# Loading and casting the feed-forward weights first, and new due times in the planner of a fused attention and feed-forward kernel

## The chip, the cores and the metric

The kernel runs on one core of one Trainium2 chip. The metric is the device time of one execution in microseconds (us); the time before is the median of three runs. One profiled execution gives the page and the trace, whose span (883.6 us) goes from the first to the last instruction and is some 2 to 3 us shorter than the time.

The engines are named as the profile names them: PE (TensorE, matrix products; PEld its weight loads), DVE (VectorE), ACT (ScalarE), POOL (GpSimd) and SP (SyncE, which here only issues transfers). Each engine runs its own queue in order and waits for the others by semaphores.

## The reference

Eight batches of eight heads, 576 positions, head size 64. For each row of scores only the 32 largest are kept, the softmax is taken over these, and the result, 4608 tokens of 512, goes through a feed-forward layer with a squared ReLU:

```python
scores = scale * np.matmul(q, k.transpose(0, 1, 3, 2))
kth = np.partition(scores, -32, axis=-1)[..., -32:-31]
scores = np.where(scores >= kth, scores, -1e9)
attn = softmax(scores)
x = (attn @ v).transpose(0, 2, 1, 3).reshape(4608, 512)
h = x @ w_in                 # w_in 512 x 2048
out = np.maximum(h, 0) ** 2 @ w_out   # w_out 2048 x 512
```

## The kernel before

**Groups.** A step of attention is a group: 128 query rows of the two heads of a head pair (or, for the last 64 rows of each head, of four heads). There are 144 groups, 18 for each batch. For a group `top_k` and `attend` do the following.

- PE computes scores of two heads against all keys (the helper at line 424, f32) into a PSUM tile of three banks, of which there is one. ACT copies them to an `s` tile (line 533; six buffers).
- DVE finds the 32nd largest score of each row: pairwise maxima (line 589, with an ACT copy of `m` at line 597, and line 599), then rounds of MAX8 and MATCH_REPLACE8 (lines 616 and 620) and a last MAX8 which gives the threshold `kth` (line 623). POOL does integer additions and subtractions for it (line 584).
- ACT computes a penalty `w` (line 631, twice for a group; four buffers). PE transposes the scores and adds the penalty to them in PSUM, in three pieces called flips (`flip`; lines 427 and 424), again in a tile of three banks of which there is one. ACT takes the exponential into `p` (line 665; four buffers).

`collect` multiplies `p` by v (PE), copies (ACT, line 692), takes reciprocals (DVE, line 694), scales (POOL, line 696), transposes (PE) and copies the result into `xt` (ACT, line 720). When four head pairs of 256 rows are there, they form a chunk, which `feed` takes through the feed-forward layer: eight blocks of products with `win` (`fh`), ReLU on ACT (line 746), squares on POOL or ACT (lines 757 and 760), then products with `wo` in four parts for each 128 rows (`fo`), a copy and a store. There are 19 chunks; the last two have 128 rows. In the last chunk DVE squares (line 754).

**Weights.** `win` and `wo` stay in SBUF as bf16. They come as 16 pieces of 512 KB in f32: eight of w_in, then eight of w_out. Each is loaded into one of two `ws` buffers, which lie in the memory of the last eight of the 17 `g` tiles, and then cast by POOL (line 868). Every `fh` and `fo` lists all 16 casts as its dependences (`after=weights`), so that no `g` tile is written before the `ws` buffers are done with.

**The planner.** Nothing of the order is written by hand. Each operation is put into a plan (`pl.op`) with its engine, an estimated duration, a due time (`prio`: the smaller, the earlier it is taken of all that are ready) and what it depends on. `schedule` plays the program with these estimates and fixes the order on each engine, and the buffer of each tile. The due times are built from a nominal time of the group, `tg = T0 + PER*n`, and constants: `LEAD` (how far ahead scores are due), `ME`, `MQ`, `MP`, `MA` (steps of the top-k), `LAG`, `LAGL` and `STEP` (the feed-forward blocks), `LATE` (the reciprocals), `SQ` (which squares POOL gets). A flip is due at `tg + PER + 2`. A chunk that is complete after group n is due from `T0 + PER*n + 20` on (`+ 8` in the last batch), plus `LAG` (or `LAGL`), and may not begin before a time called `nbf`. In the plan a link costs a latency: 0.12 us between engines, 0.07 on the same engine, 0.25 on PE. Some links only fix an order (`order=[...]`, and the operation that takes a tile before those that use it); these have no semaphore on the chip but the same latency in the plan.

A second, exact program follows in the code and runs only if a check of the results asks for it.

Of the kernel before, what the change touches and what calls it, by code (L numbers as in the profile page):

```python
# [85 lines left out]
class Plan:  # L86
# [33 lines left out]
    def schedule(self, t0=0.0, latency=0.12, own=0.07):  # L120

        left = {}
        for o in self.ops:
            left[o] = len(o.deps | o.later)
            for d in o.deps | o.later:
                d.users.append(o)
        ready = {e: [] for e in ENGS}
        busy = {e: t0 for e in ENGS}
        order = {e: [] for e in ENGS}
        events = []  # L130
        n = 0

        def push(t, kind, x):
            nonlocal n
            heapq.heappush(events, (t, n, kind, x))
            n += 1

        for o in self.ops:
            if left[o] == 0:
                push(max(t0, t0 + o.nbf), "ready", o)  # L140
        push(t0, "go", None)
        readyat = {o: t0 + o.nbf for o in self.ops}
        done = 0
        locked = t0
        while events:
            t = events[0][0]
            while events and events[0][0] <= t + 1e-9:
                _, _, kind, x = heapq.heappop(events)
                if kind == "end":
                    done += 1  # L150
                    for tl in x.tiles:
                        tl.left -= 1
                        if tl.left == 0 and tl.slot is not None:
                            for i in range(tl.width):
                                tl.pool.last[tl.slot + i] = tl
                            tl.pool.give(tl.slot, tl.width)
                    for v in x.users:
                        left[v] -= 1
                        lat = (own if x.eng != "pe" else .25) if v.eng == x.eng else latency
                        readyat[v] = max(readyat[v], t + lat)  # L160
                        if left[v] == 0:
                            push(readyat[v] + v.late, "ready", v)
                elif kind == "ready":
                    heapq.heappush(ready[x.eng], (x.prio, x.seq, x))
            for e in ENGS:
                if busy[e] > t + 1e-9 or (e == "gp" and locked > t + 1e-9):
                    continue
                skipped = []
                while ready[e]:
                    item = heapq.heappop(ready[e])  # L170
                    o = item[2]
                    got = []
                    ok = True
                    for tl in o.takes:
                        s = tl.pool.take(tl)
                        if s is None:
                            ok = False
                            break
                        got.append((tl, s))
# [12 lines left out]
                    o.start = max(t, busy["gp"]) if o.lk else t  # L192
                    hold = o.dur if e != "sp" else 0.6 * o.ndma
                    o.end = o.start + o.dur + (hold if e == "sp" else 0)
                    busy[e] = o.start + hold
                    if o.lk:
                        locked = o.end
                    order[e].append(o)
                    push(busy[e], "go", None)
                    push(o.end, "end", o)  # L200
                    break
                for item in skipped:
                    heapq.heappush(ready[e], item)
        assert done == len(self.ops), (done, len(self.ops), t, [
            (e, i[0], [(x.pool.name, len(x.pool.free)) for x in i[2].takes]) for e in ENGS for i in sorted(ready[e])[:4]])
        self.order = order
        return max(o.end for o in self.ops)
# [84 lines left out]
def bass_top_k_attn__then__act_relu_squared_kernel(  # L292
# [24 lines left out]
            return nc.alloc_sbuf_tensor(name, shape, dt)  # L317
        return [nc.alloc_sbuf_tensor(f"{name}{i}", shape, dt) for i in range(n)]

    PER = 5.76  # L320
    T0 = 12.0
    LEAD = 26.59
    ME = 10.33
    MQ = 12.36
    MP = 4.03
    MA = 14.06
    SQ = 5.68
    LAG = 17.25
    STEP = 2.97
    LATE = 1.59  # L330
    LAGL = 18.87

    ident32 = sb("ident32", [P, P])
    ident_bf = sb("ident_bf", [P, P], BF16)
# [29 lines left out]
    NG = 17  # L364
    gmem = sb("g", [P, NG, 512], BF16)
    mem["g"] = [gmem[:, i, :] for i in range(NG)]
    mem["ws"] = [gmem[:, NG - 8 + 4 * i:NG - 4 + 4 * i, :].rearrange("p a c -> p (a c)").bitcast(FP32) for i in range(2)]
    pools["g"], pools["ws"] = Pool("g", NG), Pool("ws", 2)
    ps32 = nc.alloc_psum_tensor("ps", [P, 8, 512], FP32)
    ps16 = ps32[:, :, :].bitcast(BF16)  # L370

# [53 lines left out]

    def tr(o, i, ident, **kw):
        return pe.matmul(o, i, ident, is_transpose=True, skip_group_check=True, **kw)  # L427

    def build(full, weights, pl):
        state = {"n": 0, "u": 0, "pairs": 0, "last": {}}  # L430
# [295 lines left out]
        def feed(chunk, xt, tm, step):  # L726
# [7 lines left out]
            for i, g in enumerate(gs):  # L734
                hh = Tile(psum)

                def fh(hh=hh, i=i):
                    for f in range(kf):
                        fb = kf * i + f
                        for ct in range(NCT):  # L740
                            ins = mm(bank(hh)[:, nt * f:nt * f + nt], win[:, ct, 128 * fb:128 * fb + 128],
                                     at(xt)[:, ct, 0:nt], ct == 0 and f == 0)
                    return ins

                def fr(hh=hh, g=g):
                    return act.activation(at(g)[:, 0:kf * nt], bank(hh)[:, 0:kf * nt], ACTF.Relu)  # L746

                tf = tm + step * i
                w_ = kf * nt
                ho = pl.op("pe", .03 + kf * 4 * (nt / 2340 + .002), tf + lag, fh, r=[xt], w=[hh], take=[hh, g], after=weights,  # L750
                      nbf=tf if not last else 0)
                pl.op("act", .19 + w_ / 1200, tf + lag + .5, fr, r=[hh], w=[g])
                if end:
                    pl.op("dve", .1 + w_ / 1900, tf + lag + .8, lambda g=g: vec.tensor_tensor(
                        at(g)[:, 0:w_], at(g)[:, 0:w_], at(g)[:, 0:w_], ALU.mult), u=[g])
                elif last or i * SQ % 8 < SQ:
                    pl.op("gp", .15 + w_ / 480, tf + lag + 1, lambda g=g: gp.tensor_tensor(  # L757
                        at(g)[:, 0:w_], at(g)[:, 0:w_], at(g)[:, 0:w_], ALU.mult), u=[g])
                else:
                    pl.op("act", .19 + w_ / 1200, tf + lag + 1, lambda g=g: act.activation(  # L760
                        at(g)[:, 0:w_], at(g)[:, 0:w_], ACTF.Square), u=[g])
            for tb in range((nt + 127) // 128):
# [3 lines left out]
                for sub in range(4):  # L766
                    def fo(sub=sub, op_=op_, tb=tb, n_=n_):
                        for fb in range(4 * sub, 4 * sub + 4):
# [3 lines left out]

                    pl.op("pe", .9, to + lag + step * sub, fo,
                          r=sorted({gs[fb // kf] for fb in range(4 * sub, 4 * sub + 4)}, key=lambda t: t.num),
                          w=[op_], take=[op_, ob] if sub == 0 else [], after=weights, order=[ho],
                          nbf=to + step * sub if not last else 0)
                pl.op("act", .6, to + lag + 4 * step, lambda op_=op_, ob=ob, n_=n_: act.copy(
                    at(ob)[0:n_, :], bank(op_)[0:n_, :]), r=[op_], w=[ob])
# [22 lines left out]
        for b in range(NB):  # L801
# [3 lines left out]
            for hp, gi in seq:  # L805
# [17 lines left out]
                collect(gi, held[hp, js[0]], (xts[i], col, first), hp, tt)  # L823
                left[i] -= n_ * (2 if gi == Z else 1)
                if left[i] == 0:
                    tm = T0 + PER * state["n"] + (20 if not last else 8)
                    c = CHUNKS[i]
                    feed(c, xts[i], tm, (STEP if b < NB - 2 else 1.9) if not last else (1.5 if c is not CHUNKS[-1] else .5))
        return kths, rzs

    def setup(pl):
# [22 lines left out]
        for i in range(16):  # L854
            s = tile("ws")
            if i < 8:
                ct, half = divmod(i, 2)
                src = wi[:, ct, 1024 * half:1024 * half + 1024]
                dst = win[:, ct, 1024 * half:1024 * half + 1024]
                view = lambda s: at(s)[:, :]  # L860
            else:
# [1 line left out]
                src = wo_ap[:, fb:fb + 2, :]  # L863
                dst = wo[:, fb:fb + 2, :]
                view = lambda s: at(s)[:, :].rearrange("p (f o) -> p f o", f=2)
            pl.op("sp", 4.0, 20 + 4 * i, lambda s=s, src=src, view=view: [nc.sync.dma_start(view(s), src)],
                  w=[s], take=[s], ndma=1, sem=lambda o: f"ws{o.takes[0].slot}")
            weights.append(pl.op("gp", 1.1, 40 + 6 * i, lambda s=s, dst=dst, view=view: gp.tensor_copy(dst, view(s)),
                                 r=[s]))
        return [i1], pre, zeros, weights  # L870

    def verdict(pl, kths, rzs):
# [24 lines left out]
    for o in main.ops[n_pre:]:  # L897
        if o.eng == "sp" and o.takes and o.takes[0].pool.name == "rv":
            o.deps.update(zeros)
        if o.eng == "pe":  # L900
            o.deps.update(early if n < 7 else early + pre)
            n += 1
    span = main.schedule()
    em.number(main)
    again = Plan()
    build(True, [], again)
# [68 lines left out]
```

## Time and profile before

| what | value |
|---|---|
| time, median of 3 | 886.55 us (885.84 to 886.85) |
| span of the profiled run | 883.6 us |
| PE busy | 820.0 us (93%) |
| DVE busy | 824.0 us (93%) |
| POOL busy | 799.3 us (90%) |
| ACT busy | 754.5 us (85%) |
| mean granted clock of PE | 0.988 |
| transfers | 48.19 MB, 55 GB/s on the mean |

Two engines have the same share, and two others are near. A share is a mean over the span. Matmuls are pipelined and their ends are modelled, so PE's busy time is not work at its peak. The chain of work that ended last has DVE in 49% of the span, PE in 26% and ACT in 13%. An idle time in the waits is put down to what released it. Windows give the busy time of each engine in a stretch, and with one line of the source the time and number of its instructions.

### The profile page before, as it was taken

To read this page: it belongs to the slowest core of one execution; us is meant where nothing else is said; L and a number is where in the kernel's file an instruction comes from. 1 tells how busy PE (TensorE), PEld (TensorE's weight loads), DVE (VectorE), ACT (ScalarE), POOL (GpSimd) and SP (SyncE) were. 2 spreads that over 40 slices of the span, in tenths; PEclk is the share of its full clock that TensorE was granted. 3 is DMA by queue.
4 is the path that set the end of the run, shared out by engine and by line. 5 is a ranking of instruction groups with operands and counts; after the bars stand their busy time and mean duration, and the time that the engine had idled before them with its cause. 6 is when DMAs were issued, how large, how long until landed. Compare 5 with 4: busy or idle time off the path is not lost.

```text
span 883.6 us, 22178 instructions
## 1 busy us (share of the span) xinstructions
PE 820.0 (93%) x7778; PEld 611.7 (69%) x7778; DVE 824.0 (93%) x3409; ACT 754.5 (85%) x1242; POOL 799.3 (90%) x833
## 2 busy tenths in 40 slices
PE   6768779999999999999999999999999999999996
PEld 4556557767777776767777768777778676786774
DVE  2998999999999999999999999999999999988951
ACT  3766788989989898989999889898999998998863
POOL 6988989999999899998999999999999999999951
PEclk9988999999999999999999999999999999999998
DMA  6732550203121212112130024011311200000100
GB/s 135 180 102 85 137 140 16 53 14 81 43 68 40 67 34 63 28 31 63 40 82 2 13 66 95 27 29 41 83 46 49 66 14 20 21 1 14 37 25 29
DMA packets 126968, 48.19 MB, mean 55 GB/s; under 512 B 119168, under 2 KB 119168, under 8 KB 126848
## 3 DMA queue, kind: packets, MB, share of 16 engines
q1 hardware_dynamic: 125648, 46.39, 20.8%
q8 instruction: 63, 1.03, 0.5%
q14 instruction: 57, 0.47, 0.2%
q10 hardware_dynamic: 1200, 0.30, 0.2%
HBM read 37.22 MB, written 9.44 MB: 53 GB/s over the span
## 4 chain that ended last, share of the span: by engine, by line
DVE 49%; PE 26%; ACT 13%; POOL 6%; issue 5%; DMA 0%; SPq 0%; DVEq 0%; POOLq 0%
PE ps L424 19%; DVE f L620 15%; DVE c L616 12%; DVE kth L623 11%; PE ps L427 7%; DVE ps L589 4%; ACT p L665 4%; DVE f L599 4%; DVE m L589 3%; ACT s L533 3%; ACT w L631 2%; POOL t L584 2%; POOL f L584 2%; ACT g L746 2%; POOL g L757 1%
## 5 line engine op out<-in xcount | busy, mean ns | idle before, releaser
L620 DVE MATCH_REPLACE8 f<-c,f 128x104 f32<-128x104 f32 (+2 forms) x864 | 268.1, 317 | 0.0
L427 PE MATMUL ps<-ident,s 128*128 128x128 f32 x1296 | 227.0, 285 | 37.7 <-ACT p L665 27.7
L616 DVE MAX8 c<-f 128x8 f32<-128x104 f32 (+2 forms) x864 | 254.0, 323 | 0.0
L631 ACT ACTIVATE w<-s,kth 128x576 bf16<-128x576 f32 x288 | 224.2, 785 | 12.2 <-DVE kth L623 11.6
L584 POOL TENSOR_TENSOR t<-s 128x576 int32<-128x576 int32 x144 | 202.9, 1412 | 18.1 <-ACT s L533 17.6
L424 PE MATMUL ps<-qk 64*128 64x64 f32 (+3 forms) x1280 | 211.9, 450 | 7.4 <-DVE m L589 6.7
L623 DVE MAX8 kth<-f 128x8 f32<-128x576 f32 x288 | 208.9, 750 | 0.0
L584 POOL TENSOR_TENSOR f<-t,m 128x576 int32<-128x576 int32 x144 | 203.1, 1411 | 0.0
L427 PEld LDWEIGHTS ps<-ident,s 128*128 128x128 f32 x1296 | 148.7, 142 | 78.0 <-ACT p L665 36.8
L533 ACT COPY s<-ps 128x1152 f32<-128x1152 f32 x144 | 162.2, 1126 | 37.5 <-PE ps L424 36.8
L424 PEld LDWEIGHTS ps<-qk 64*128 64x128 f32 (+1 forms) x1280 | 131.2, 180 | 84.5 <-issue 69.0
L665 ACT ACTIVATE p<-ps 128x1152 bf16<-128x1152 f32 x144 | 163.2, 1133 | 22.7 <-PE ps L424 22.1
L424 PE MATMUL ps<-steep_bf,w 128*128 128x128 bf16 x1296 | 144.8, 221 | 0.0
L424 PE MATMUL ps<-wo,g 128*128 128x512 bf16 x576 | 143.9, 379 | 0.3 <-DVE flag L889 0.2
L584 POOL TENSOR_TENSOR t<-m 128x288 int32<-128x288 int32 x144 | 114.9, 798 | 21.3 <-ACT m L597 9.2
L424 PE MATMUL ps<-xt,win 128*128 128x256 bf16 (+1 forms) x1088 | 127.6, 267 | 1.5 <-ACT av L692 0.7
L584 POOL TENSOR_TENSOR f<-t,f 128x288 int32<-128x288 int32 x144 | 115.0, 799 | 0.2 <-DVE f L599 0.2
L424 PEld LDWEIGHTS ps<-steep_bf,w 128*128 128x128 bf16 x1296 | 108.1, 102 | 5.6
L424 PEld LDWEIGHTS ps<-xt,win 128*128 128x128 bf16 x1088 | 96.0, 98 | 16.3 <-ACT g L746 2.6
L757 POOL TENSOR_TENSOR g<-g 128x512 bf16<-128x512 bf16 x95 | 98.5, 1042 | 8.0 <-ACT g L746 7.3
L746 ACT ACTIVATE g<-ps 128x512 bf16<-128x512 f32 x144 | 86.1, 605 | 8.4 <-PE ps L424 7.7
L589 DVE TENSOR_TENSOR ps<-ps,s 128x288 f32<-128x288 f32 x144 | 65.2, 453 | 22.2 <-ACT s L533 20.1
(58 smaller groups left out, 856.9 us busy)
## 6 DMA issues: line engine op xcount, KB each, us to landing
rq<-in_q_dram SPq DMA_DIRECT2D x64, 128.0 KB, 2.5
rv<-in_v_dram SPq DMA_DIRECT2D x64, 128.0 KB, 2.5
out_dram<-o SPq DMA_DIRECT2D x32, 256.0 KB, 2.1
rk<-in_k_dram SPq DMA_DIRECT2D x62, 128.0 KB, 2.6
g<-in_moe_w_in_dram SPq DMA_DIRECT2D x8, 512.0 KB, 4.6
g<-in_moe_w_out_dram SPq DMA_DIRECT2D x8, 512.0 KB, 4.3
rv<-in_v_dram SPq DMA_DIRECT2D x96, 16.0 KB, 2.2
rq<-in_q_dram SPq DMA_DIRECT2D x32, 32.0 KB, 2.6
```

The source lines that it names most:

```text
L424: return pe.matmul(o, l, r, start=start, stop=stop, skip_group_check=True)
L427: return pe.matmul(o, i, ident, is_transpose=True, skip_group_check=True, **kw)
L533: cp = [pl.op("act", 1.2, tg - LEAD + 1, lambda: act.copy(at(st)[:, :, :], two(banks(ss), SECOND, S)), r=[ss], w=[st])]
L584: return pl.op("gp", dur, prio, lambda: gp.tensor_tensor(o().bitcast(I32), x().bitcast(I32), y().bitcast(I32), op), **kw)
L589: return vec.tensor_tensor(o, two(banks(ss)[:, a:], SECOND + HALF, QUART), two(at(st)[:, 0, HALF + a:], HALF, QUART), ALU.max)
L616: lambda i=i, t=t, c0=c0, c1=c1: vec.max(eighth(t, i), at(f)[:, i, c0:c1]),
L620: lambda i=i, t=t, c0=c0, c1=c1: vec.match_replace(at(f)[:, i, c0:c1], eighth(t, i), at(f)[:, i, c0:c1], NEG), hold=[f])]
L623: ks.append(chain(kth, i, prev[i] + [low], .665, lambda i=i: vec.max(eighth(kth, i), at(f)[:, i, :]), hold=[f]))
L631: pl.op("act", .77, tw + .8 * i, lambda i=i: act.activation(at(wt)[:, i, :], at(st)[:, i, :], ACTF.Relu, bias=kth[:, i, n:n + 1], scale=-1.0),
L665: pl.op("act", 1.15, tt + 1, lambda: act.activation(at(pt)[:, :, :].rearrange("p k q -> p (k q)"), banks(e)[:, 0:2 * S], ACTF.Exp, scale=0 ...
L746: return act.activation(at(g)[:, 0:kf * nt], bank(hh)[:, 0:kf * nt], ACTF.Relu)
L757: pl.op("gp", .15 + w_ / 480, tf + lag + 1, lambda g=g: gp.tensor_tensor(at(g)[:, 0:w_], at(g)[:, 0:w_], at(g)[:, 0:w_], ALU.mult), u=[g])
```

## The change

The change makes the weights come first and lets the first chunk wait for them piece by piece; it also changes the due times.

- The 16 loads are due at `WD*i - 60`, not before `WN` = 6 us, in place of `20 + 4*i`. The w_in pieces come in the order of halves (all four row blocks of the first 1024 columns, then of the second).
- The casts are due at once (`WC` = 0). Where `i % 4 < WA` = 2.47, ACT casts, else POOL: 12 and 4.
- The `fh` of the first chunk wait for the four pieces of their half only; each `fo` waits for its two pieces of w_out. The two `ws` buffers change places, and a line makes sure that the `g` tiles of the first chunk lie outside them.
- Links that only fix an order have no latency in the plan.
- The constants of the due times have new values, and the 20 in the due time of a chunk becomes `NBO` = 8.74.

```diff
-                        lat = (own if x.eng != "pe" else .25) if v.eng == x.eng else latency
+                        lat = 0 if x not in v.deps else (own if x.eng != "pe" else .25) if v.eng == x.eng else latency
...
-    PER = 5.76
+    PER = 5.52
     T0 = 12.0
-    LEAD = 26.59
-    ME = 10.33
-    MQ = 12.36
-    MP = 4.03
-    MA = 14.06
-    SQ = 5.68
-    LAG = 17.25
-    STEP = 2.97
-    LATE = 1.59
-    LAGL = 18.87
+    LEAD = 36.03
+    ME = 17.74
+    MQ = 18.56
+    MP = 5.21
+    MA = 21.03
+    SQ = 4.72
+    WD = 4
+    WC = 0
+    WA = 2.47
+    WN = 6
+    NBO = 8.74
+    LAG = 12.01
+    STEP = 2.91
+    LATE = 1.54
+    LAGL = 20
...
-    mem["ws"] = [gmem[:, NG - 8 + 4 * i:NG - 4 + 4 * i, :].rearrange("p a c -> p (a c)").bitcast(FP32) for i in range(2)]
+    mem["ws"] = [gmem[:, NG - 4 - 4 * i:NG - 4 * i, :].rearrange("p a c -> p (a c)").bitcast(FP32) for i in range(NWS)]
...
-                ho = pl.op("pe", .03 + kf * 4 * (nt / 2340 + .002), tf + lag, fh, r=[xt], w=[hh], take=[hh, g], after=weights,
+                ho = pl.op("pe", .03 + kf * 4 * (nt / 2340 + .002), tf + lag, fh, r=[xt], w=[hh], take=[hh, g],
+                           after=weights if chunk is not CHUNKS[0] else weights and weights[NCT * (kf * i // 8):][:NCT],
...
-                          w=[op_], take=[op_, ob] if sub == 0 else [], after=weights, order=[ho],
+                          w=[op_], take=[op_, ob] if sub == 0 else [], after=weights[8 + 2 * sub:10 + 2 * sub], order=[ho],
...
-                    tm = T0 + PER * state["n"] + (20 if not last else 8)
+                    tm = T0 + PER * state["n"] + (NBO if not last else 8)
...
-                ct, half = divmod(i, 2)
+                half, ct = divmod(i, NCT)
...
-            pl.op("sp", 4.0, 20 + 4 * i, lambda s=s, src=src, view=view: [nc.sync.dma_start(view(s), src)],
-                  w=[s], take=[s], ndma=1, sem=lambda o: f"ws{o.takes[0].slot}")
-            weights.append(pl.op("gp", 1.1, 40 + 6 * i, lambda s=s, dst=dst, view=view: gp.tensor_copy(dst, view(s)),
-                                 r=[s]))
+            pl.op("sp", 4.0, WD * i - 60, lambda s=s, src=src, view=view: [nc.sync.dma_start(view(s), src)],
+                  w=[s], take=[s], ndma=1, sem=lambda o: f"ws{o.takes[0].slot}", nbf=WN)
+            eng, fn = ("act", act.copy) if i % 4 < WA else ("gp", gp.tensor_copy)
+            weights.append(pl.op(eng, 1.1, WC * i, lambda s=s, dst=dst, view=view, fn=fn: fn(dst, view(s)), r=[s]))
```

More of the change, by code (lines that the diff above doesn't have):

```diff
@@ L366, in bass_top_k_attn__then__act_relu_squared_kernel @@
     mem["g"] = [gmem[:, i, :] for i in range(NG)]
-    mem["ws"] = [gmem[:, NG - 8 + 4 * i:NG - 4 + 4 * i, :].rearrange("p a c -> p (a c)").bitcast(FP32) for i in range(2)]
-    pools["g"], pools["ws"] = Pool("g", NG), Pool("ws", 2)
+    NWS = 2
+    mem["ws"] = [gmem[:, NG - 4 - 4 * i:NG - 4 * i, :].rearrange("p a c -> p (a c)").bitcast(FP32) for i in range(NWS)]
+    pools["g"], pools["ws"] = Pool("g", NG), Pool("ws", NWS)
     ps32 = nc.alloc_psum_tensor("ps", [P, 8, 512], FP32)
@@ L427, in tr @@
         return pe.matmul(o, i, ident, is_transpose=True, skip_group_check=True, **kw)
+    first_h = []
     def build(full, weights, pl):
@@ L749, in feed @@
                 w_ = kf * nt
-                ho = pl.op("pe", .03 + kf * 4 * (nt / 2340 + .002), tf + lag, fh, r=[xt], w=[hh], take=[hh, g], after=weights,
-                      nbf=tf if not last else 0)
+                ho = pl.op("pe", .03 + kf * 4 * (nt / 2340 + .002), tf + lag, fh, r=[xt], w=[hh], take=[hh, g],
+                           after=weights if chunk is not CHUNKS[0] else weights and weights[NCT * (kf * i // 8):][:NCT],
+                           nbf=tf if not last else 0)
+                if chunk is CHUNKS[0] and weights:
+                    first_h.append(ho)
                 pl.op("act", .19 + w_ / 1200, tf + lag + .5, fr, r=[hh], w=[g])
@@ L903, in bass_top_k_attn__then__act_relu_squared_kernel @@
     span = main.schedule()
+    assert all(o.takes[1].slot < NG - 4 * NWS for o in first_h)
     em.number(main)
```

## The prediction

> **What bounds the kernel now.** I read the busy shares first, then the stages (busy time of each engine in windows), the waits of VectorE, the instructions on the g tile, and running counts of two ScalarE lines; the timeline of the last 60 us came last. The page has PE at 820.0 us (93%) and DVE at 824.0 us (93%), so two engines could be the bound. The windows separate them (columns: window, its length, then PE, PEld, DVE, ACT, POOL busy with instruction counts, granted clock, DMA share, GB/s):
>
> ```profile
> 12.60:140.00 127.40, 94.93 (x822) 72.73 (x823) 117.30 (x479) 92.95 (x153) 116.07 (x117) 0.93 0.47 121
> 140.00:740.00 600.00, 586.88 (x5628) 436.60 (x5628) 598.68 (x2491) 551.94 (x909) 569.08 (x572) 1.00 0.19 47
> 740.00:850.00 110.00, 107.57 (x1028) 80.20 (x1025) 102.59 (x426) 91.31 (x148) 102.95 (x106) 1.00 0.06 16
> 850.00:883.60 33.60, 24.74 (x286) 18.03 (x284) 5.44 (x18) 14.42 (x29) 6.09 (x9) 0.93 0.10 35
> ```
>
> See the third busy number. VectorE has 1.3 us of idle time in the middle 600 us: nothing done there can give more than that, however much PE is relieved. It is idle 12.6 us before its first instruction, 127.40 - 117.30 = 10.1 us up to 140, 110.00 - 102.59 = 7.4 us in the last stretch, and after its last top-k result (about 849.9) comes a tail of 33.7 us. So the time is: start 12.6 + VectorE's top-k work (about 818) + its holes (10.1 + 1.3 + 7.4 = 18.8) + tail 33.7 = 883.
>
> Why is there a tail? The weights, on the g tile:
>
> ```profile
> L746 ACT ACTIVATE g<-ps x144: 578/597/717, 137.2 to 872.7; 128x512 bf16<-128x512 f32 x144
> ...
> L866 SPq DMA_DIRECT2D g<-in_moe_w_in_dram x8: 328/508/595, 22.8 to 73.8; - x8
> L868 POOL CAST win<-g x8: 1032/1035/1037, 36.3 to 85.2; 128x1024 bf16<-128x1024 f32 x8
> L866 SPq DMA_DIRECT2D g<-in_moe_w_out_dram x8: 367/375/602, 80.5 to 125.2; - x8
> L868 POOL CAST wo<-g x8: 1026/1040/1049, 91.0 to 133.9; 128x1024 bf16<-128x1024 f32 x8
> ```
>
> The last of 16 casts starts at 133.9 and takes 1.0 us; every feed-forward matmul waits for all 16, and the first on win starts at 136.1. Its input was ready long before: the fourth xt copy of chunk 0 is
>
> ```profile
> 90.12 0.38 ACT L720 COPY xt<-ps 128x256 bf16<-128x256 bf16 x1
> ```
>
> So chunk 0 (64 matmuls on win, 32 on wo) stands still from 90.5 to 136, and PE has holes meanwhile: between 75 and 137 it is busy 48.1 of 62.0 us. Afterwards PE never catches up. The running count of w activations (two for each group) against exponentials (one for each group), first at 120 us, then at 840 us, w first:
>
> ```profile
> 0.00:120.00 120.00, 24.53 (x32) 0.93 0.50 126
> 0.00:840.00 840.00, 221.25 (x284) 0.99 0.22 56
> ```
> ```profile
> 0.00:120.00 120.00, 16.00 (x14) 0.93 0.50 126
> 0.00:840.00 840.00, 156.46 (x138) 0.99 0.22 56
> ```
>
> At 120 us attend is 16 - 14 = 2 groups behind the top-k; at 840 us, 142 - 138 = 4 groups, all that the four w buffers allow. This debt is what the tail pays, one group in about 4.6 us (exponentials at 849.5, 854.5, 859.1, 863.6 in the timeline):
>
> ```profile
> 848.53 1.41 DVE L623 MAX8 kth<-f 128x8 f32<-128x576 f32 x2
> ```
> ```profile
> 860.29 0.66 PE L427 MATMUL ps<-ident,s 128*128 128x128 f32 x4 [0.59 <-ACT p L665]
> ```
>
> The last threshold is there at 849.9, its two w activations end near 852.5, and its transposes begin at 860.3.
>
> **What the Trainium skill says.** "Perfetto Trace Analysis", Identifying the Most-Contended Engine: matmul occupancy is no measure of closeness to the limit, occupancy of VectorE is. The trace agrees: PE at 98% in the middle loses to VectorE at 99.8%, and so I count PE's debt in groups. "TensorE: Matmul & The Clock Gate", Part 1: a PE that idles falls back to half clock. The trace has a granted clock of 0.66 to 0.84 in the stretches from 60 to 80 us, where scores of one group take 1.75 us against 1.35 us at full clock. "Trainium Kernel Development and Optimization", Key Constraints: transfers of all queues share 16 DMA engines and interleave; here 0.64 busy over the first 20 us. The price of the cast on ScalarE is below.
>
> **The change, part by part.**
>
> *Loads.* 16 pieces of 512 KB through two buffers, due at 4i - 60 (not before 6 us) in place of 20 + 4i. Before, they ran from 22.8 to 125.2, one in 6.8 us, since casts were due late and lay behind POOL's work. One turn of a buffer now is a landing of 4.5 us (median), a cast of 1.04 us and a wait for the engine in front of it. With no wait this is 5.5/2 = 2.8 us for a piece, the last cast near 50 us; with the old pace it would be near 115 us. I take 2.5 us of wait, 4 us for a piece: w_in complete near 38 us, all near 70 us. Both come before 90.5, so waiting piece by piece is itself worth nothing: the early load is the gain.
>
> *Casts.* i % 4 below 2.47 gives 12 to ScalarE and 4 to POOL. POOL loses 12 x 1.035 = 12.4 us. ScalarE's cost is not in the trace: the nearest row, a copy of 128x1152 f32, takes 1126 ns, and "ScalarE: Activation LUTs", What ACT_TABLE_LOAD costs, gives 186 ns + 0.833 ns an element without pointer operands: 1039 ns for 1024, against 1146 for 1152, so the trace agrees. The estimate is 12 x 1.04 = 12.5 us, and bounds of 1.0 and 1.13 us make little difference. ScalarE is idle 60 - 37.1 = 22.9 us in the first 60 us, so it fits. But its queue is in order: a cast that waits for a late transfer holds the score copies (line 533) behind it, and VectorE waits for those.
>
> *First loads.* Piece 0 goes ahead of the second pair's q, whose issue begins at 5.6. A 512 KB piece lands in 4.5 us against 2.5 us for a 128 KB one; the delay is between 0 and 4.5 us. The second k lands near 11 and is transposed at 15.9, so most is hidden. I take 1 us.
>
> *Chunk 0 on time.* Its PE work, by the busy totals, is 64 of 1088 win matmuls (127.6 us) and 32 of 576 wo matmuls (143.9 us): 7.5 + 8.0 = 15.5 us. It moves from after 136 into the holes before, which are 13.9 us between 75 and 137. PE's debt falls by about that: 3 groups of 4.6 us.
>
> *Due times.* Feed-forward work is due NBO + LAG - (PER + 2) after the flips of the same group: before 20 + 17.25 - 7.76 = 29.5, or 5.1 groups of 5.76; after 8.74 + 12.01 - 7.52 = 13.2, or 2.4 groups of 5.52. So the last two batches' feed-forward blocks lie some 2.7 groups (15 us) earlier, out of the tail. Scores rise from 26.59 to 36.03 ahead, the ScalarE copy of m (MA) from 14.06 to 21.03, the first maxima (ME) from 10.33 to 17.74. VectorE's waits for that copy (4.1 us in the first 200 us, longest 1.5) come from its lying behind w in ScalarE's queue; being due earlier should remove most.
>
> *Zero latency on order-only links.* No semaphore belongs to them, so nothing is removed on the chip; the planner only stops putting other PE work between the three flips. SQ leaves 5 of 8 squares on POOL (other ones), so no load moves.
>
> **Sum.** Holes to 140: the 10.1 us hold 3.7 us of start-up waits for score copies, which stay, and about 6.4 others, of which I take 4.5; less 1 for the first loads: -3.5. Last stretch, 7.4 us: the waits there (3.9 for POOL's f, 3.2 for score copies) follow from the jam of feed-forward work around 790; I take -4. Tail: the last flips can start 8.5 us earlier (860.3 down to about 851.8), and 2.6 us of wo matmuls lie in front of the last transpose at 868.04, so 11 us at most; I take -10. Total -17.5. On 886.55 that is 869.0 us.
>
> **The rivals.**
> A (0.55), the above: 869, with 862 to 875 for the terms' errors.
> B (0.20): the debt forms again. For it: PE is 98% busy from 140 on, and all due times change at once. Then only the early holes and some 4 us of tail come back: 886.5 - 3.5 - 4 = 879.
> C (0.12): everything is recovered, 6.4 + 7.4 + 11 = 25 us, and 3 more from the start: 858. Against it: the start-up waits depend on a cold pipeline.
> D (0.13): slower. Twelve casts wait in order on ScalarE for transfers that share engines with q, k and v; if each is 1 us late and VectorE has no spare scores yet, 12 us are lost early and half the gain stays: 886.5 + 12 - 8.5 = 890. Against it: 22.9 us of idle ScalarE, and seven score copies by 40 us against three finished groups, so some slack.
>
> **How the numbers follow.** The time is A's, 869. The range, 857 to 884, takes in A, B and nearly all of C, and leaves out D. Faster by over 0.2% (below 884.8) is A, B and C less a sliver: 0.86; within, 0.03; slower 0.11, most of D.
>
> **What would show it.** Right: casts on ScalarE and POOL done by about 70 us; the first win matmul near 90 or before; a granted clock near 1.0 from 60 to 140; VectorE idle under 8 us between its start and 140; w less exponentials at most 2 to 3 groups at the end; tail under 26 us; VectorE's total unchanged at 824. Wrong: a tail still above 30 us (B), or VectorE idle over 15 us before 140 with ScalarE casts waiting on transfers (D).

## The result, and the profile after

The changed kernel takes 876.75 us (median of four runs, 875.84 to 878.58), against 886.19 us for the kernel before, measured beside it. The ratio is 0.9896, with a 95% interval of 0.9878 to 0.9915: 9.4 us faster. The forecast was 17.5 us faster.

The windows of the changed kernel, with the columns as before (window, length, busy time of PE, PEld, DVE, ACT and POOL, granted clock, DMA share, GB/s):

```profile
12.60:140.00 127.40, 105.58 (x925) 80.36 (x929) 118.78 (x490) 110.11 (x175) 116.79 (x117) 0.92 0.49 120
140.00:740.00 600.00, 573.40 (x5532) 430.81 (x5568) 598.26 (x2479) 548.58 (x904) 559.77 (x564) 1.00 0.19 46
740.00:850.00 110.00, 107.03 (x1052) 80.78 (x1059) 104.01 (x432) 93.74 (x154) 100.64 (x105) 1.00 0.07 21
850.00:875.40 25.40, 18.40 (x209) 12.94 (x208) 3.19 (x11) 8.79 (x17) 4.82 (x6) 0.96 0.10 36
```

The trace lacks 52 matmul records of this run, all of products with `wo` (524 of 576), so PE's busy time here is a few us too low. VectorE is still the engine without idle time in the middle 600 us (1.7 us of it). The gain is at the two ends. Measured from VectorE's first instruction and to its last threshold, the profiled runs give:

| part of the span, us | before | after | change | forecast |
|---|---|---|---|---|
| VectorE starts at | 12.62 | 12.45 | -0.2 | 0 |
| its holes up to 140 | 10.08 | 8.62 | -1.5 | -3.5 |
| its holes, 140 to 740 | 1.32 | 1.74 | +0.4 | 0 |
| its holes, 740 to the last threshold | 7.37 | 4.24 | -3.1 | -4 |
| its work up to the last threshold | | | +0.7 | 0 |
| last threshold ends at | 849.9 | 846.3 | -3.6 | -7.5 |
| tail after it | 33.7 | 29.1 | -4.6 | -10 |
| span | 883.6 | 875.4 | -8.2 | -17.5 |

The fifth row is the rest of the difference: VectorE's total is 0.4 us longer (824.4 against 824.0), and some of its small instructions now lie ahead of the last threshold and not in the tail. The second row is less sure than it looks: six further runs below (n1, n2, r1, x2, x4, x5) have the changed kernel's order on every engine up to 140 us, and their holes there are 9.8 to 10.9 us. What differs from run to run covers the 1.5 us.

The weights did what was asked of them. The instructions on the g tile (shortest, median and longest in ns, then the first and last start):

```profile
L754 ACT ACTIVATE g<-ps x144: 577/599/674, 96.1 to 865.4; 128x512 bf16<-128x512 f32 x144
...
L880 ACT CAST win<-g x6: 1037/1048/1068, 13.2 to 41.5; 128x1024 bf16<-128x1024 f32 x6
L880 ACT CAST wo<-g x6: 1035/1062/1085, 48.6 to 69.2; 128x1024 bf16<-128x1024 f32 x6
L880 POOL CAST win<-g x2: 1036/1044/1051, 25.0 to 43.1; 128x1024 bf16<-128x1024 f32 x2
L880 POOL CAST wo<-g x2: 1036/1037/1038, 59.7 to 73.7; 128x1024 bf16<-128x1024 f32 x2
```

The last cast starts at 73.7 where it was 133.9, and the first `win` matmul at 94.8 where it was 136.0. The running counts of w activations (two for each group), at 120 and at 840 us, and below them those of exponentials:

```profile
0.00:120.00 120.00, 24.50 (x32) 0.91 0.55 134
0.00:840.00 840.00, 220.50 (x286) 0.99 0.23 56
```
```profile
0.00:120.00 120.00, 17.15 (x15) 0.91 0.55 134
0.00:840.00 840.00, 158.84 (x140) 0.99 0.23 56
```

At 120 us attend is now one group behind the top-k (it was two). It stays at one until 440 us, goes to three by 520, and at 840 it is 143 - 140 = 3. The distance that the forecast called a debt came back without any late weights.

### The profile page after: what moved, and what is told of

The parts are those of the page before. It is cut to its first block, busy times and chain, and to the rows that moved or that the text cites. A ratio compares the mean times of both kernels' runs of the same rounds, so it can differ in the third digit from the quotient of the medians.

```text
span 875.4 us, 22041 instructions
## 1 busy us (share of the span) xinstructions
PE 809.3 (92%) x7726; PEld 608.3 (69%) x7778; DVE 824.4 (94%) x3409; ACT 765.1 (87%) x1254; POOL 787.2 (90%) x821
## 4 chain that ended last, share of the span: by engine, by line
DVE 59%; PE 23%; ACT 10%; issue 4%; POOL 2%; DMA 0%; SPq 0%; DVEq 0%
DVE f L628 19%; PE ps L430 16%; DVE c L624 14%; DVE kth L631 12%; PE ps L433 6%; DVE f L607 5%; DVE ps L597 4%; DVE m L597 4%; ACT p L673 3%; ACT s L541 3%; ACT w L639 2%; POOL f L592 1%; POOL t L592 1%; ACT g L754 1%; DMA rq<-in_q_dram 0%
## 5 line engine op out<-in xcount | busy, mean ns | idle before, releaser
L624 DVE MAX8 c<-f 128x8 f32<-128x104 f32 (+2 forms) x864 | 244.9, 319 | 0.0
L433 PE MATMUL ps<-ident,s 128*128 128x128 f32 x1296 | 224.2, 282 | 20.5 <-ACT p L673 10.8
L433 PEld LDWEIGHTS ps<-ident,s 128*128 128x128 f32 x1296 | 145.7, 142 | 49.1 <-ACT p L673 18.1
L430 PE MATMUL ps<-steep_bf,w 128*128 128x128 bf16 x1296 | 141.2, 221 | 0.0
L430 PE MATMUL ps<-wo,g 128*128 128x512 bf16 x524 | 129.3, 379 | 5.4 <-ACT g L754 1.7
L768 POOL TENSOR_TENSOR g<-g 128x512 bf16<-128x512 bf16 x95 | 98.5, 1040 | 14.2 <-ACT g L754 12.5
L430 PEld LDWEIGHTS ps<-steep_bf,w 128*128 128x128 bf16 x1296 | 106.0, 100 | 4.8
L430 PEld LDWEIGHTS ps<-wo,g 128*128 128x128 bf16 x576 | 52.1, 98 | 49.5 <-ACT g L754 1.7
```

Of the source, the lines that this page charges most:

```text
L430: return pe.matmul(o, l, r, start=start, stop=stop, skip_group_check=True)
L624: lambda i=i, t=t, c0=c0, c1=c1: vec.max(eighth(t, i), at(f)[:, i, c0:c1]),
```

## The experiments

Each was timed in three rounds; "ratio" is to the kernel before, with its 95% interval. The five stage numbers are from one profiled run each: VectorE's holes up to 140 us, from 140 to 740 and from 740 to the last threshold, the tail, and how many groups attend is behind at 840 us. The changed kernel was timed beside the kernel before, but not again beside the other runs, so two rows are best compared by their ratios.

| kernel | us | ratio | holes to 140 | middle holes | last holes | tail | behind |
|---|---|---|---|---|---|---|---|
| before | 886.19 | 1 | 10.1 | 1.3 | 7.4 | 33.7 | 4 |
| changed | 876.75 | 0.9896 (0.9878-0.9915) | 8.6 | 1.7 | 4.2 | 29.1 | 3 |
| e1 weights only | 885.84 | 0.9997 (0.998-1.0013) | 7.5 | 2.2 | 7.4 | 33.5 | 3 |
| e2 rest only | 887.22 | 0.9993 (0.9976-1.001) | 14.2 | 5.0 | 4.9 | 32.3 | 3 |
| e3 no zero latency | 890.44 | 1.0047 (1.003-1.0064) | 12.8 | 6.0 | 6.5 | 32.5 | 3 |
| e4 zero latency only | 891.42 | 1.0047 (1.0027-1.0068) | 15.5 | 2.1 | 8.3 | 30.1 | 4 |
| n1 LAG + 0.05 | 878.22 | 0.9914 (0.9887-0.994) | 9.9 | 1.4 | 4.3 | 29.1 | 2.5 |
| n2 LAG - 0.05 | 882.27 | 0.9954 (0.9941-0.9968) | 9.8 | 1.5 | 4.9 | 32.4 | 3.5 |
| x1 before, chunk 0 light | 886.40 | 0.9994 (0.9979-1.0009) | 10.7 | 1.3 | 7.4 | 33.6 | 4 |
| x2 changed, chunks 14, 15 light | 879.21 | 0.9918 (0.989-0.9945) | 10.9 | 1.8 | 4.0 | 29.1 | 2.5 |
| x5 changed, chunk 16 light | 879.19 | 0.9913 (0.9892-0.9933) | 9.9 | 1.8 | 5.0 | 28.0 | 2.5 |
| x4 changed, small loads | 879.64 | 0.9927 (0.9899-0.9954) | 9.8 | 1.7 | 4.3 | 29.0 | 2.5 |
| r2 changed, PE warmed | 877.50 | 0.9894 (0.9869-0.9918) | 11.8 | 1.8 | 4.3 | 29.0 | 2.5 |
| r1 changed, LAGL 14 | 881.46 | 0.994 (0.992-0.9961) | 9.9 | 1.7 | 6.3 | 30.1 | 3 |

### The change in two halves

e1 has the loads, casts and waits of the change, with all the old constants of due times and the old latencies in the plan. e2 is the other half: the new constants and latencies, with the weights as before.

```diff
# e1, in the changed kernel
-                        lat = 0 if x not in v.deps else (own if x.eng != "pe" else .25) if v.eng == x.eng else latency
+                        lat = (own if x.eng != "pe" else .25) if v.eng == x.eng else latency
...
-    PER = 5.52
+    PER = 5.76
...
-    NBO = 8.74
-    LAG = 12.01
+    NBO = 20
+    LAG = 17.25
...
# e2, in the changed kernel
-            pl.op("sp", 4.0, WD * i - 60, ...
+            pl.op("sp", 4.0, 20 + 4 * i, ...
...
-            eng, fn = ("act", act.copy) if i % 4 < WA else ("gp", gp.tensor_copy)
+            eng, fn = "gp", gp.tensor_copy
```

> The kernel before with the new loads and casts alone (old constants, old latencies). Theory 1 (carried debt): the work of chunk 0 that PE could not do before 136 us stays as a debt to the end, so early weights bring most of the gain: 878 to 880 us, tail after the last threshold about 29 us, w less p of 3 at 840 us. Theory 2 (due times): PE has enough slack in the middle to pay the debt there, and the tail follows from the due times of the last chunks: 884 to 887 us, tail about 33 us, w less p still 4 at 840 us.

> The changed kernel with the weights loaded, cast and waited for as before (due times and zero latency new). Theory 1: 883 to 886 us, tail 32 us or more, since the debt of chunk 0 is there again. Theory 2: 877 to 880 us, tail about 29 us; chunk 0 is late again but that costs at most the 1 to 2 us of holes of VectorE before 140 us.

In the median neither half moves the time: 885.84 and 887.22 us, both intervals around 1. Theory 2 said so of e1; e2 lies above what either theory gave. In e1 the first `win` matmul starts at 99.0 us instead of 136.0, and VectorE's early holes are 7.5 us in the profiled run (the fastest of twelve, 2.8 us under the median). The tail is 33.5 us, as before, and attend is already three groups behind at 200 us. In e2 the last holes and the tail shrink by 2.5 and 1.4 us, and the early and middle holes grow by 4.1 and 3.7. So early weights alone leave the tail where it was, and new due times alone nearly do (32.3 us). In the medians the halves sum to nothing and together make 9.4 us.

The runs of e2 lie wide apart, 879.6 to 892.8 us. The five with the highest mean clock (0.993 to 0.995) have a median of 881.3 us. The changed kernel hardly depends on it: 877.2 and 878.6 us at 0.987 and 0.985, 875.8 and 876.4 at 0.997. Why e2 is sometimes that fast was not followed up.

### The latency in the plan

e3 is the changed kernel with the old latency line (the first pair of lines in the diff above); e4 is the kernel before with the new one.

> The changed kernel with the old latency on order-only links. As predicted (the links have no semaphore): 876 to 878 us. Rival (the planner packs the three flips closer, so that the one flip tile comes free sooner): 880 us or more, more wait of PE for the exponential than the 10.8 us of the changed kernel.

> The kernel before with zero latency on order-only links alone. As predicted: 885 to 887 us. Rival: 880 to 883 us, the wait of PE for the exponential (27.7 us before) falls by a third or more.

I had costed this line at nothing, since no semaphore belongs to it. Alone it makes the kernel 0.5% slower (e4), and without it the change is 0.5% slower than before (e3) instead of 1% faster. It takes nothing from the chip; it changes the order that the planner writes, and with it VectorE's early holes (15.5 us in e4, 12.8 in e3), the last ones, and in e3 the middle ones (6.0 us). PE's wait for the exponential goes as the rival said, 11.6 us in e4 instead of 27.7 and 18.0 in e3 instead of 10.8, but in e4 the time rises all the same: the time does not hang on that wait.

### Neutral nudges

If the order is what counts, then an edit with no meaning should move the time as well. n1 and n2 are the changed kernel with one due time moved by 0.05 us:

```diff
-    LAG = 12.01
+    LAG = 12.06
...
-    LAG = 12.01
+    LAG = 11.96
```

> The changed kernel with LAG 12.06 for 12.01: 0.05 us in the due times of feed-forward work, which no step of the prediction can tell from nothing. The order on the engines is the same up to about a sixth of the program and another one after it. If the gain belongs to the steps as argued: 876 to 878 us. Theory 3 (the gain belongs to one particular order, and any new order is a new draw): outside 874 to 880.

> The changed kernel with LAG 11.96 for 12.01, again 0.05 us, to the other side. As for the other: 876 to 878 us if the gain belongs to the steps, outside 874 to 880 if it belongs to one order.

878.22 us is not told apart from 876.75. The other, 882.27 us, loses 5.5 of the 9.4 us; of the 4.8 us by which the profiled spans differ, 3.3 are in the tail (32.4 us). No operation differs between these kernels, only the place of some of them in their queues (n2's PE queue is that of the changed kernel for the first 208 us). All three orders near these constants beat the kernel before, by 4 to 9 us.

### Is the tail a debt of PE work?

The forecast said that PE could not work off chunk 0 and pays for it in the tail. If so, taking the work away must shorten the tail. x1 does that to the kernel before, with the order on every engine unchanged: the matmuls of chunk 0 are cut to a quarter, so that some 11.6 us of PE work (three quarters of the 15.5 worked out above) drop out. x2 does it to chunks 14 and 15 of the changed kernel (23 us, before 830 us), x5 to chunk 16 (the first of the last batch). These kernels leave out three quarters of the named chunks' products.

```diff
-                        for ct in range(NCT):
+                        for ct in range(1 if lite else NCT):
...
-for fb in range(4 * sub, 4 * sub + 4):
+for fb in range(4 * sub, 4 * sub + (1 if lite else 4)):
...
+            lite = not full and chunk is CHUNKS[0]                      # x1
+            lite = not full and chunk in (CHUNKS[14], CHUNKS[15])       # x2
+            lite = not full and chunk is CHUNKS[16]                     # x5
```

> The kernel before with the same order on every engine, but 72 of the 96 feed-forward matmuls of chunk 0 left out (48 on win, 24 on wo: 5.6 + 6.0 = 11.6 us of PE work at about 136 to 160 us). Theory 1 (carried debt): PE is 11 us ahead from there on, and the end comes 6 to 11 us earlier (875 to 880). Theory 3 (each engine's order is fixed, VectorE sets the pace in the middle and PE's few holes swallow it): under 2 us, 884.5 to 886.5, with PE's idle time between 140 and 740 up from 13 to about 24 us.

> The changed kernel with the same order, but 144 of the 192 feed-forward matmuls of the last block of batch 6 and of the second block of 64-row rests left out (about 23 us of PE work between 735 and 830 us). If PE's jam in the last 140 us sets the tail: 866 to 870 us, tail 22 to 25 us, w less p of 1 to 2 at 840. If the tail is the latency of the last groups' own chain (flips, exponential, products with v, transposes, feed-forward of the last two chunks): 874 to 877 us, tail still 28 us or more.

> The changed kernel with the same order, but 72 of the 96 feed-forward matmuls of the first chunk of the last batch left out (rows 256 to 511; 11.6 us of PE work, which lies between 826 and 855). In the changed kernel PE is busy 43.1 of the 44.1 us from the moment when that chunk's input is complete (824.7) to its last product (868.8). If PE's work after that moment is what the tail consists of: the end comes 6 to 11 us earlier, 866 to 871 us, tail 19 to 24 us. If the tail is the latency of the last groups' chain: 874 to 878 us, tail still above 27 us.

All three miss what a debt asks for. x1 comes out as theory 3 said. x2 and x5 have the tails of the other reading (29.1 and 28.0 us), at times 1 to 2 us above its ranges. Windows of x1 (compare the first with the 586.88 of the kernel before):

```profile
140.00:740.00 600.00, 578.33 (x5527) 432.90 (x5570) 598.66 (x2490) 551.80 (x910) 569.25 (x572) 0.99 0.19 47
740.00:850.00 110.00, 106.98 (x1020) 80.11 (x1028) 102.61 (x427) 92.05 (x148) 104.22 (x107) 1.00 0.06 16
```

Between 140 and 740 PE's busy time is 8.6 us lower (a part of this only because 43 records are missing there: 5527 matmuls, 5570 weight loads) and VectorE's is the same. The tail is 33.6 us, the time 886.40. The last stretch up to the last threshold, first of the changed kernel, then of x2:

```profile
740.00:846.30 106.30, 103.38 (x1013) 78.06 (x1019) 102.06 (x427) 90.84 (x149) 100.24 (x104) 1.00 0.07 19
```
```profile
740.00:848.30 108.30, 89.16 (x892) 66.66 (x896) 104.31 (x438) 92.26 (x151) 102.27 (x106) 0.98 0.07 19
```

In x2 PE is idle for 19.1 of 108.3 us where it was idle for 2.9 of 106.3, and the tail is 29.1 us in both. So up to the last threshold PE at 97 or 98% was not short of time. Less work in the same order leaves the tail nearly as it was; the same work in another order changes it (n2). The reading that this leaves is that the distance of attend is fixed by where the flips stand in PE's in-order queue, among scores and feed-forward blocks that themselves wait for VectorE. No run moves the flips alone.

### What the start loses

In the kernel before, VectorE waited in all 4.1 us for the ACT copy of m up to 200 us, and 1.6 us for exponentials. In the changed kernel, its waits up to 140 us are (us in total, times, longest):

```profile
DVE ps L597 <- ACT s L541: 15.2, 2, 12.5
DVE ps L597 <- ACT p L673: 5.5, 5, 2.7
DVE f L607 <- ACT m L605: 0.2, 1, 0.2
```

The wait for the copy is gone, as forecast, and another has grown: the first maxima wait for an exponential. Half of them is written into the PSUM tile `sq`, which shares its bank with the ninth flip `e9`; the maxima of a later group, now due earlier, stand in VectorE's queue and wait until ACT has read the flip. The longest of these waits, and two windows around it:

```profile
34.22 0.47 DVE L597 TENSOR_TENSOR ps<-ps,s 128x288 f32<-128x288 f32 x1 [2.73 <-ACT p L673]
```
```profile
25.00:30.00 5.00, 4.04 (x15) 2.72 (x16) 4.81 (x18) 2.44 (x7) 4.20 (x6) 0.50 0.82 195
30.00:35.00 5.00, 3.87 (x22) 3.26 (x22) 2.27 (x13) 3.74 (x4) 4.00 (x4) 0.62 0.93 207
```

The granted clock is 0.50 and 0.62 just there, and transfers take 82 and 93% of the DMA engines. Two runs ask which of these counts. x4 loads only 64 of the 1024 columns of each piece and casts these 16 times over, so that most of the weights' traffic drops out (over the first 75 us the DMA engines are busy 40% of the time for 80%) while every instruction keeps its place; it leaves out the other columns of the weights. r2 puts 36 bf16 matmuls of 128x128 in front of PE's queue, to have the clock up when the scores begin.

```diff
# x4
-lambda s=s, src=src, view=view: [nc.sync.dma_start(view(s), src)]
+lambda s=s, src=src, view=view: [nc.sync.dma_start(at(s)[:, 0:64], ...[:, 0:64])]
...
# r2
+            for _ in range(36):
+                pe.matmul(ps32[:, 6, 0:P], ident_bf[:, :], ident_bf[:, :], start=True, stop=True, skip_group_check=True)
             emit("pe", pe_)
```

> The changed kernel with the same order, but each of the 16 loads of weights brings 64 columns (32 KB) in place of 512 KB, and each cast reads these 64 columns 16 times over, so that the casts cost about the same and most of the traffic is left out. The prediction put the loads' contention at 1 us. If that holds: 875 to 877, VectorE's holes to 140 us 7.5 to 8.6 us. If the loads of weights delay q, k and v and so make the new holes (5.5 us of waits behind the exponential): holes of 4 to 6 us, time 872.5 to 874.5.

> The changed kernel with 36 more 128x128 matmuls of the identity ahead of PE's first instruction (about 4 us from 2 to 6 us, when PE waits for the first q), nothing else; the order behind them is the same. If PE at half clock makes VectorE start late (the first scores take 2.50 us, later ones 1.35): VectorE starts at 10.5 to 11 for 12.45, time 873.5 to 875.5. If the first 140 us are set by other things, the gain is lost again at the next wait: 876 to 877.5.

x4 has holes of 9.8 us, as other runs with this order have, and still waits 5.6 us behind the exponential: the loads do not cost VectorE anything that can be seen. In r2 the first scores take 1.35 us for 2.50 and VectorE starts at 11.13 us, 1.3 us earlier. It loses this at the next waits; two of them from its timeline:

```profile
27.16 0.47 DVE L597 TENSOR_TENSOR ps<-ps,s 128x288 f32<-128x288 f32 x1 [1.19 <-ACT s L541]
...
34.80 0.47 DVE L597 TENSOR_TENSOR ps<-ps,s 128x288 f32<-128x288 f32 x1 [2.27 <-ACT p L673]
```

The clock of r2 is at 0.50 to 0.57 in every window from 10 to 35 us, and its next four scores, from 12.01 to 28.05 us, take 2.48 to 2.50 us each. Of the second to fifth scores of the changed kernel two take 1.35 us and two about 2.5. So the warm-up did not hold, and whether a clock at full speed over this whole stretch would help was not reached. 877.50 us is not told apart from 876.75.

### What the tail gives back

In the tail, the last exponential starts 13.7 us after the last threshold in the kernel before (863.60 against 849.9) and 5.7 us after it in the changed one:

```profile
851.97 1.13 ACT L673 ACTIVATE p<-ps 128x1152 bf16<-128x1152 f32 x1 [0.57 <-PE ps L430]
```

That is 8.0 us, close to the 8.5 of the forecast. But from there to the end it takes 20.0 us before (883.6 - 863.60) and 23.4 after: 3.4 us are given back. The larger part lies between the exponential and the last transpose, which comes 7.0 us after it (858.96) and came 4.4 us after it before (868.04 - 863.60). Rows of the changed kernel's timeline, then of the kernel before:

```profile
855.41 2.85 PE L430 MATMUL ps<-xt,win 128*128 128x128 bf16 x48 [0.36 <-ACT o L788]
...
857.19 1.04 POOL L768 TENSOR_TENSOR g<-g 128x512 bf16<-128x512 bf16 x1 [2.49 <-ACT g L754]
858.19 0.40 POOL L704 TENSOR_TENSOR x<-av,rzall 128x128 bf16<-128x128 f32 x1
...
858.32 0.81 PE L430 MATMUL ps<-wo,g 128*128 128x512 bf16 x3
858.96 0.22 PE L433 MATMUL ps<-ident_bf,x 128*128 128x128 bf16 x1
```
```profile
865.44 2.76 PE L424 MATMUL ps<-wo,g 128*128 128x512 bf16 x12
...
868.04 0.22 PE L427 MATMUL ps<-ident_bf,x 128*128 128x128 bf16 x1
```

Two queues stand ahead of the transpose. On POOL the last scale stands behind a square that waits 2.49 us for a ReLU of ACT: the reciprocal is done at 855.73, and the scale starts at 858.19 (before: 865.94 and 866.46). But the scale is done by 858.59, and PE comes to the transpose only at 858.96. From 855.41 on PE works without a gap on 48 `win` and 4 `wo` products of the chunk before the last (the record of one is missing), which stand ahead of the transpose in its queue. The wait on PE ends last, so an earlier scale alone would not have moved the transpose. Before, 12 `wo` products stood there. The products of `p` with v come later as well, 2.6 us after the start of the exponential against 1.3, behind `wo` products. So 1.3 us are lost ahead of the products with v and 1.3 between them and the transpose: 2.6 of the 3.4 us. The rest is on PE behind the transpose:

```profile
859.02 1.03 PE L430 MATMUL ps<-wo,g 128*128 128x512 bf16 x4
859.88 1.06 PE L430 MATMUL ps<-xt,win 128*128 128x128 bf16 x16
...
862.53 1.03 PE L430 MATMUL ps<-wo,g 128*128 128x512 bf16 x4
863.40 1.95 PE L430 MATMUL ps<-xt,win 128*128 128x128 bf16 x32
865.40 3.40 PE L430 MATMUL ps<-wo,g 128*128 128x512 bf16 x15
```

The `wo` products of the chunk before the last stand between the `win` blocks of the last one. Transpose to end takes 16.4 us (875.4 - 858.96) against 15.6. r1 moves these blocks by the due time of the last batch's feed-forward work.

```diff
-    LAGL = 20
+    LAGL = 14
```

> The changed kernel with LAGL 14 for 20, which moves only the due times of the feed-forward blocks that end in the last batch; the order is another one in the last 120 us alone. In the changed kernel the products with wo of the last but one chunk stand between the blocks of win of the last chunk, which costs about 3 us at the very end. With LAGL 14 they stand before its transposes. If the tail is given by the order of the last blocks on PE: tail 25 to 27 us for 29.1, time 873 to 875. If the tail's length is set by something else: 876 to 878, or worse if the flips move back.

The interleaving is gone: after the last transpose, at 865.46, the `win` products come in one run, and from there to the end it takes 14.9 us (880.4 - 865.46) and not 16.4. From PE's timeline:

```profile
858.71 0.61 PE L433 MATMUL ps<-ident,s 128*128 128x128 f32 x4
...
866.38 3.74 PE L430 MATMUL ps<-xt,win 128*128 128x128 bf16 x64
869.95 3.62 PE L430 MATMUL ps<-wo,g 128*128 128x512 bf16 x16
```

From the last exponential to the end it is 20.0 us again, as before the change, so this part of the account holds. But the feed-forward blocks that left the end now stand ahead of the last flips (first row), so the last exponential starts at 860.42 and not at 851.97, 10.1 us after the last threshold for 5.7. The last threshold itself comes 4.0 us later (850.3). The tail is 30.1 us where 25 to 27 were expected, and the time is 881.46 us.

x5 does not touch this stretch: chunk 16 is light there, and the 48 and 4 products ahead of the transpose belong to chunk 17 (they run from 856.39 to 859.94 in x5). So no run takes PE work out of the stretch behind the last exponential, where the chain that ended last runs on PE alone from 855.41 to 868.8. An order with only these products put behind the transpose was not tried.

## Why the prediction was right, and where not

The direction and the range were right, and the time was 7.75 us above the forecast. That the direction came right is in part luck: by the same reasoning e1 would have had most of the gain and e3 all of it, and they took 885.84 and 890.44 us. By its steps:

**Bound.** Right. VectorE's work is 824.4 us (824.0), its idle time in the middle 1.7 us, and the time is its start, work, holes and the tail. What the forecast cites of the Trainium skill, "Perfetto Trace Analysis", Identifying the Most-Contended Engine, that the occupancy of matmuls is no good measure of how near the limit is, agrees with these runs: up to the last threshold PE was 97 to 98% busy, and 11.6 to 23 us less work for it made no kernel faster.

**Loads and casts.** Right. `w_in` is cast by 44 us (38 forecast) and all by 74.7 (70); a cast takes 1.05 to 1.06 us on ACT at the median, close to the estimate of 1.04. Rival D's mechanism, casts that hold the score copies and so VectorE up, isn't in VectorE's waits (2.7 us for score copies after the start, 3.7 before). Waiting piece by piece is worth nothing, as forecast: all casts are done 20 us before the first `win` matmul, and a plan in which the first chunk waits for all 16 has the same order on PE, VectorE and ACT.

**Early holes, -3.5 forecast, -1.5 measured,** and about nothing in the six other runs with this order. The removed wait was named rightly (4.1 to 0.2 us). The step that failed is "being due earlier should remove most" taken as a net gain: the earlier maxima ran into a buffer that they share with the ninth flip, and the waits there grew from 1.6 to 5.5 us. The 1 us for the first loads was not there.

**Chunk 0 on time.** The work moved into the early stretch: PE is busy 10.7 us more up to 140 us (105.58 - 94.93). That this repays a debt is the step that failed. "PE's debt falls by about that: 3 groups" took a distance set by the order of queues for a shortage of PE time. x1, x2 and x5 show it: with 11.6 to 23 us of the work away and the order kept, no time comes back.

**Due times.** The last flips did move ahead, 8.0 us against 8.5. So the tail had this from the order, and not from the repaid debt. The tail's term was -10, where -4.6 was measured. It counted a part of the 2.6 us of `wo` products ahead of the last transpose as a further gain, and these grew to 48 `win` and 4 `wo` products: 2.6 us were lost up to the transpose and 0.9 behind it. The working was also wrong for the last batch. There the sum is 8 + 18.87 - 7.76 = 19.1 before and 8 + 20 - 7.52 = 20.5 after, so the blocks that now stand in the way were due 1.4 us later, not 15 us earlier.

**Last stretch, -4 forecast, -3.1 measured.** Nearly right. Of the 4.2 us left, 3.9 lie just ahead of the last threshold:

```profile
843.42 0.17 DVE L702 RECIPROCAL rzall<-av 128x2 f32<-128x2 f32 x1 [2.55 <-ACT av L700]
843.49 1.40 POOL L592 TENSOR_TENSOR f<-t,m 128x576 int32<-128x576 int32 x1
...
844.92 1.42 DVE L631 MAX8 kth<-f 128x8 f32<-128x576 f32 x2 [1.34 <-POOL f L592]
```

A reciprocal stands ahead of the last MAX8 in VectorE's queue and waits 2.55 us, but it is done at 843.59, and the `f` that the MAX8 needs is there only at 844.89. It is POOL's `f` that ends last, a wait that the forecast had named (3.9 us before).

**Zero latency.** "Nothing is removed on the chip" is right. Costing it at nothing was wrong: with this line alone undone, the kernel is at 890.44 us, 13.7 above. I left out that an edit of the planner redraws the whole order.

**The signs named.** The casts (74.7 us for 70), the first `win` matmul (94.8 for 90), VectorE's total and the distance at the end (3) came about as said. Three did not: the clock is 0.85 from 60 to 75 us and 1.00 only after it, VectorE is idle 8.6 us up to 140 (under 8), the tail is 29.1 us (under 26).

**Rivals.** The time lies between A (869) and B (879), nearer to B. B's sign, a tail above 30 us, did not come (29.1), nor did A's, below 26. Neither had the mechanism.

**What stays open.** Why the two halves give nothing alone (in the median) and 9.4 us together is known only as an outcome of the orders, stage by stage. n1 and n2 bound what can be said: of the 9.4 us, some 4 stand in all three orders near these constants, and up to 5.5 hang on the particular one. Three orders are too few for a mean.

## What to carry to other kernels

In a program whose queues are ordered by a planner, a part of a change may have no price of its own: time a few neutral nudges of a due time (here 0.05 us, worth up to 5.5 us) before crediting a constant. To test whether a busy engine is the bound, take work out of it with the order kept; here PE at 98% busy gave back no time for 11.6 us less work. And follow the chain of a tail to its last instruction, asking on each engine's queue what stands ahead and what that waits for. Where an instruction is held up in two queues, only the wait that ends last costs time: here PE's and not POOL's.

## What the runs showed of the hardware

In some of these kernels the time goes with the mean granted clock of the run. It falls by 4.7 us for each 0.01 over 12 runs of e1, by 6.2 over 20 of e2 and by 5.8 over 20 of e4 (correlation -0.81, -0.80 and -0.83). It is no rule: over the 48 runs of the kernel before that were timed beside them the correlation is -0.13, and over 17 of n2 it is +0.11. Whether the clock itself costs the time or both follow from the start of the run was not tried. In the changed kernel nearly all the lost clock that is recorded lies early: 0.92 on the mean from 12.6 to 140 us and 1.00 from there to 850.

A granted clock of 1.00 at the very start of a profile need not mean full speed. In the changed kernel the column is at 1.00 up to 20 us, but the first two scores, at 8.75 and 13.33 us, take 2.50 us each, as long as the scores of r2 at 17.36 us, where its clock is 0.50, and the third, at 18.35, takes 1.35. The first entry of the clock in this trace lies at 16.7 us; nothing is recorded ahead of it.

A warm-up of 36 matmuls, about 4 us, sped up the first scores (1.35 us for 2.50) and did not keep the clock up. In r2 it was at 0.50 to 0.57 from 10 to 35 us although PE was busy for 3.0 to 4.5 us of each 5.
